# Polysketch attention and a multiplicative feed-forward block: the same 1179 steps dealt out in another order, with half of the first keys and S transferred first

## The chip, the cores and the metric

The kernel runs on one core of one Trainium2 chip. A core has five engines that matter here: TensorE (PE, the matmuls), VectorE (DVE), ScalarE (ACT), GpSimd (POOL) and SyncE (SP, which in this kernel only issues transfers). Each engine works through its own list of instructions in the order in which they stand, and waits on semaphores where it needs another engine's or a transfer's result. The metric is the device time of one execution in microseconds, as a median of several. Numbers of the trace come from one profiled execution, whose clock starts at the first instruction.

## The reference

```python
def phi(x):                                        # r = 8
    a = np.einsum('rd,bhsd->bhsr', S1, x)
    b = np.einsum('rd,bhsd->bhsr', S2, x)
    return np.einsum('bhsi,bhsj->bhsij', a, b).reshape(*x.shape[:-1], r * r)
q_p, k_p = (phi(q), phi(k))                        # q, k, v: (4, 4, 1088, 32)
kv = np.einsum('bhsf,bhsd->bhfd', k_p, v)
z = np.sum(k_p, axis=2)
num = np.einsum('bhsf,bhfd->bhsd', q_p, kv)
den = np.einsum('bhsf,bhf->bhs', q_p, z)[..., None] + 1e-06
attn = (num / den).astype(np.float32)
x = attn.transpose(0, 2, 1, 3).reshape(4 * 1088, 128)
h = (x @ w1) * (x @ w2) @ w3                       # w1, w2: 128 x 1024; w3: 1024 x 1024
out = (h @ w_out).astype(np.float32)               # w_out: 1024 x 128
```

The four batches are independent in the attention part; the feed-forward part treats all 4352 rows of x alike. The weights arrive as double-precision words and are turned into single precision in the kernel.

## The kernel before

`make_steps` defines 1179 small named steps, each of one or a few instructions. The names say what a step belongs to:

- `k0` to `k3` are the keys of the four batches. The biggest magnitude of a batch is found on ACT (`max`, L207), the keys are split into a leading part on a grid and a rest (`lead`, `rest`, L651), a Gram matrix is made of them on PE (`gram`, L659), and from it the sums `N` that later steps need; beside that the keys are transposed (`tr`, `kT`), multiplied with S (`ab`), squared into their 64 features (`kp`, L677), and multiplied with the values (`kv0` to `kv3`, L769, and `kvr`).
- `q0` to `q6` and `qr` are pieces of the queries: projections, the features `phi` (L1208, L1509), the denominator `rc`, and at the end `xT`, the transposed rows x. `q0` and `q1` are 512 rows of batch 0 each, made in another way than the later ones.
- `w0` to `w10` turn the weights into single precision (`c` and `m` on ACT, `j` on DVE, `a` on POOL), and `f0` to `f7` multiply w3 with w_out once (L534), so that the feed-forward part is only (x w1)(x w2) w3o.
- `g0` to `g3` are the feed-forward part for 512 rows each of batches 0 and 1: `a` (L1799) and `b` (L1809) are matmuls against a 128-column block of w1 and of w2, `c` (L1804) copies the first product out of PSUM, `m` (L1815) multiplies the two on DVE, and `o` (L1835) is the matmul with w3o. `gr` is the same for the 256 rows that are left of all batches, with `o` at L1824 and `oT` at L1858.
- `h4` and `h6` are the feed-forward part of batches 2 and 3, 1024 rows each, by a scheme of seven half-size products in place of eight. The products `a1` to `a7` use rows 0 to 63 of the PE array and `b1` to `b7` rows 64 to 127 (L1673); `P1` to `P7` use columns 0 to 63 or 64 to 127 (L1759). Two neighbours on opposite halves run side by side. Copies (L1680), additions (L1685), multiplications (L1707, L1712) and sums (L1727 to L1742) on ACT, DVE and POOL stand between `a`/`b` and `P`, and a chain of DVE additions `k2` to `k9` (L1776 to L1785) ends it.
- `warm0` to `warm11` are filler matmuls on zeros (L255), 53 in all, 27 of them in `warm0`.

What sets the order of the work is a table written out by hand or by a planner: the string `ORDER` lists all step names once. The steps are traced in that order, and every instruction is chained behind the one traced before it on the same engine (L1892 to L1904), so `ORDER` fixes the list of each of the five engines. Three sets of names choose an engine: a step in `POOL` runs on GpSimd and otherwise on VectorE; a PSUM copy in `CPV` runs on VectorE and otherwise on ScalarE. `SLOTS` deals the buffers: for each kind of tile it is a string in which the n-th character says which buffer the n-th tile of the kind takes, so a step may have to wait for the last reader of that buffer.

Transfers are issued from SP, but for the two halves of batch 0's keys (`k0.load0`, `k0.load1`, L560), which are issued from ACT. Each big transfer on SP waits until the one four places ahead of it has landed (`UNDER_WAY`), and every transfer waits for the one eight places before it, since transfers share eight semaphores.

## Time and profile before

| what | value |
|---|---|
| median of 3 runs | 245.85 us (245.68 to 246.19) |
| the profiled execution's span, first to last instruction | 244.1 us |
| median less span: what lies around it | 1.75 us |
| PE busy | 236.2 us, 97% of the span |
| DVE busy | 206.7 us, 85% |
| POOL busy | 161.9 us, 66% |
| ACT busy | 123.5 us, 51% |
| mean granted TensorE clock | 0.998 |
| first matmul of the feed-forward part (`g0.4a`) | starts at 27.42 us |
| last `a`/`b`/`o` matmul ends | about 240.6 us |

The page cuts the span into 40 slices with the busy share of each engine in tenths, names the chain of work that ended last, and lists the costliest groups of instructions by source line. A table by windows of time gives the busy time of each engine in each stretch; the timeline lists the instructions one by one with the idle time ahead of each and what ended it ("issue" is idle time for which the profile shows no waited-for event). A PE record's end is modelled; how long a matmul holds the array is read from the start of the next one.

### The profile page before, as it was taken

The page shows a single profiled execution, that of the slowest core. Times are in us where ns is not written, and L with a number is a line of the kernel's source. Part 1 is how long each engine was busy: PE and PEld are TensorE (multiplying, and loading weights), DVE is VectorE, ACT ScalarE, POOL GpSimd, SP SyncE. Part 2 cuts the span into 40 slices and gives each one's busy share as a digit, 9 for nine tenths or more (in the row PEclk, how much of TensorE's full clock was granted, in tenths as well). Part 3 has the DMA queues.
Part 4 walks back from the last instruction along what each step waited for, and adds up shares of the span by engine and source line. Part 5 has one row for each costly group of instructions (what it writes and reads, how often), then busy time and mean ns, then how long its engine had stood idle before and what let it go on. Part 6 is the DMA issues. An engine that isn't in the chain of part 4 may idle for free.

```text
span 244.1 us, 6745 instructions
## 1 busy us (share of the span) xinstructions
PE 236.2 (97%) x2724; PEld 129.8 (53%) x2724; DVE 206.7 (85%) x421; ACT 123.5 (51%) x246; POOL 161.9 (66%) x203
## 2 busy tenths in 40 slices
...
GB/s 201 265 143 325 181 227 190 6 197 224 220 141 251 188 217 190 59 1 3 3 0 0 4 0 3 59 113 3 1 0 0 0 3 0 0 1 3 12 90 93
DMA packets 31935, 22.06 MB, mean 90 GB/s; under 512 B 21280, under 2 KB 26528, under 8 KB 31904
## 3 DMA queue, kind: packets, MB, share of 16 engines
...
q8 instruction: 21, 0.34, 0.6%
q10 hardware_dynamic: 544, 0.52, 0.6%
...
## 4 chain that ended last, share of the span: by engine, by line
PE 87%; DMA 5%; ACT 2%; POOL 2%; DVE 1%; issue 1%; POOLq 0%; SPq 0%
PE b_ps L1809 12%; PE ps_o L1835 12%; PE ps_X L1673 11%; PE a_ps L1799 11%; PE ps_o L1759 10%; PE ps_w3o L534 6%; PE ps_Y L1673 6%; PE ps_Z L1673 3%; PE ps_g L659 2%; PE ps_x L1527 2%; PE ps_ac L1374 2%; DMA qh<-in_q_dram 2%; DMA k<-in_k_dram 2%; PE ps_or L1824 2%; POOL ph L1208 1%; PE idle_ps L255 1%
## 5 line engine op out<-in xcount | busy, mean ns | idle before, releaser
L1673 PE MATMUL ps_X<-xd,wv 64*128 64x512 f32 x112 | 36.3, 593 | 0.0
L1799 PE MATMUL a_ps<-xT,w 128*128 128x512 f32 (+1 forms) x80 | 36.1, 562 | 0.0
L1809 PE MATMUL b_ps<-xT,w 128*128 128x512 f32 (+1 forms) x80 | 35.6, 555 | 0.0
L1804 ACT COPY ffa<-a_ps 128x512 f32<-128x512 f32 (+1 forms) x38 | 20.1, 540 | 29.2 <-PE a_ps L1799 26.7
L1707 POOL TENSOR_TENSOR hc<-hc 128x512 f32<-128x512 f32 x16 | 20.7, 1304 | 15.7 <-DVE hc L1685 15.5
L1835 PE MATMUL ps_o<-ab,w3o 128*128 128x512 f32 x64 | 29.6, 600 | 0.0
L1680 ACT COPY hc<-ps_X 128x512 f32<-128x512 f32 x38 | 21.3, 590 | 16.1 <-PE ps_X L1673 12.9
L1815 DVE TENSOR_TENSOR ab<-ffa,b_ps 128x512 f32<-128x512 f32 (+1 forms) x40 | 23.9, 623 | 4.9 <-PE b_ps L1809 4.1
L501 POOL TENSOR_TENSOR w3c<-w3c,cv_m 128x512 int32<-128x512 int32 x16 | 21.2, 1344 | 4.2 <-DVE w3c L495 4.1
L1673 PEld LDWEIGHTS ps_X<-xd,wv 64*128 64x128 f32 x112 | 14.9, 186 | 13.1 <-issue 10.9
L1799 PEld LDWEIGHTS a_ps<-xT,w 128*128 128x128 f32 x80 | 14.1, 189 | 13.9 <-issue 8.8
L1809 PEld LDWEIGHTS b_ps<-xT,w 128*128 128x128 f32 x80 | 14.4, 190 | 13.1 <-issue 8.1
L1673 PE MATMUL ps_Y<-xd,wv 64*128 64x512 f32 x48 | 19.7, 594 | 0.0
L1835 PEld LDWEIGHTS ps_o<-ab,w3o 128*128 128x128 f32 x64 | 11.6, 190 | 13.4 <-issue 13.0
L534 PEld LDWEIGHTS ps_w3o<-wo,w3T 128*128 128x128 f32 x128 | 15.3, 192 | 2.4 <-issue 2.4
L534 PE MATMUL ps_w3o<-wo,w3T 128*128 128x128 f32 x128 | 15.7, 276 | 0.0
L1759 PE MATMUL ps_o<-hc,w3o 128*64 128x512 f32 x32 | 15.1, 595 | 0.0
L1759 PE MATMUL ps_o<-tt,ws 128*64 128x512 f32 x32 | 13.7, 594 | 0.0
L1680 ACT COPY hc<-ps_Y 128x512 f32<-128x512 f32 x14 | 8.1, 592 | 9.7 <-PE ps_Y L1673 6.6
L263 ACT ACTIVATE cv_c<-raw 128x1024 f32<-128x1024 f32 (+1 forms) x13 | 13.0, 1014 | 0.0
L1540 ACT COPY xd<-ps_x 64x256 f32<-64x256 f32 x24 | 8.8, 367 | 7.2 <-PE ps_o L1835 6.8
...
## 6 DMA issues: line engine op xcount, KB each, us to landing
...
raw<-in_moe_w_dram SPq DMA_DIRECT2D x4, 512.0 KB, 5.8
...
k<-in_k_dram SPq DMA_DIRECT2D x3, 512.0 KB, 5.1
v<-in_v_dram SPq DMA_DIRECT2D x2, 512.0 KB, 6.1
...
```

What stands on the lines that cost most here:

```text
L263: act.activation(dst, hi.bitcast(F32), ACT.Prelu, scale=2.0 ** -112, alpha=-2.0 ** 32)
L501: pool.tensor_tensor(d, d, x["m"][:, i * 512:(i + 1) * 512], ALU.add)
L534: pe.matmul(t["o"], w3T[ko][:, c], wo[:, c], start=c == 0, stop=c == NC - 1)
L1673: pe.matmul(x[bank], stat(j, u)[:, i * 128:(i + 1) * 128], rows(j, u), start=new, stop=True, tile_position=(u * 64, 0), skip_group_check=True)
L1680: cp(n(y))(x[k], x[bank])
L1707: on(f"h{g}.{i}m{k}").tensor_mul(both[0][k], both[0][k], both[1][k])
L1759: pe.matmul(acc_o[bank][half[0]:half[1]], w(i), x(i), start=n == 1, stop=n == (2 if j == 3 else 4), tile_position=(0, half[0]), skip_group ...
L1799: pe.matmul(x["a"][:, :w], w_of(0, c), xT[g][:, c0:c0 + w], start=True, stop=True)
L1804: cp(f"g{g}.{c}{su}c")(x["s"][:, :w], x["a"][:, :w])
L1809: pe.matmul(x["b"][:, :w], w_of(1, c), xT[g][:, c0:c0 + w], start=True, stop=True)
L1815: dve.tensor_mul(ab_sb[g, c][:, c0:c0 + w], x["s"][:, :w], x["b"][:, :w])
L1835: pe.matmul(o_ps[g], w3o[:, c], ab_sb[g, c], start=n == 1, stop=n == NC)
```

## The change

The code of the steps is the same. What differs is six of the strings of `SLOTS`, the sets `POOL` (90 names before, 88 now: 32 left, 30 joined) and `CPV` (17 before, 20 now), and the whole of `ORDER`, which holds the same 1179 names in another order. The number of fillers is the same, too.

```diff
 SLOTS = {
     "b": 
-        "012345670214657210671306537457462512346127340273014526045721472352140327540542370673245716"
...
+        "012345670123457361203270534526506451021657206572143063275430125416214572614576305416273054"
...
-    "q_m": "0110110",
-    "raw": "010212120211221",
-    "s": "012345671252360063202461521024214",
-    "x": "012012201110",
+    "q_m": "0101101",
+    "raw": "012010201210210",
+    "s": "012345674062315470625130724635017",
+    "x": "012101201201",
...
 POOL = set("""
-    g4.oS g5.oS g6.oS g7.oS h4.0T1 h4.0T2 h4.0T3 h4.0m12 h4.0m22 h4.1T2 h4.1m11 h4.1m12 h4.2m11
-    h4.2m12 h4.2m22 h4.3m11 h4.s2 h4.s4 h6.0T2 h6.0m11 h6.0m12 h6.0m22 h6.1T2 h6.1T3 h6.1m11 h6.1m12
-    h6.1m22 h6.2T1 h6.2T4 h6.2m11 h6.3T3 h6.3m11 h6.s1 h6.s2 h6.s4 k0.Nf k0.Nh k0.Nr k0.kp1 k1.Nr
-    k1.kp1 k2.kp0 k2.kp1 k2.rest0 k3.kp0 k3.kp1 q0.al q0.p01 q0.phi1 q0.sca q1.al q1.bs q1.p12
-    q1.phi q1.sca q2.bs q2.p2 q2.phi0 q2.sc q2.sl q3.al q3.bs q3.p01 q3.p12 q3.p2 q3.phi0 q3.sc
-    q4.al q4.bs q4.nn q4.p01 q4.p2 q4.phi0 q4.sl q6.al q6.nn q6.p01 q6.phi1 q6.sc q6.sl qr.al qr.bs
-    qr.p12 qr.p2 s.KS s.Pp s.blk s.blkh s.low s.rest
+    g4.oS g5.oS g6.oS g7.oS h4.0T1 h4.0T3 h4.0T4 h4.0m12 h4.0m22 h4.1T1 h4.1T3 h4.1m11 h4.1m12
+    h4.1m22 h4.2m11 h4.2m12 h4.s2 h6.0m11 h6.0m12 h6.0m22 h6.1T1 h6.1T3 h6.1T4 h6.1m12 h6.1m22
+    h6.2T2 h6.2T3 h6.2m12 h6.2m22 h6.s1 h6.s2 h6.s4 k0.Nf k0.Nh k0.rest1 k1.Nr k1.kp0 k1.kp1
+    k1.rest0 k2.Nr k2.kp1 k2.rest0 k3.Nr k3.rest0 q0.al q0.p2 q0.phi1 q0.sca q1.al q1.bs q1.p12
+    q1.p2 q1.phi q2.al q2.bs q2.p12 q2.p2 q2.phi0 q2.sc q2.sl q3.al q3.bs q3.p12 q3.sc q3.sl q4.bs
+    q4.nm q4.nn q4.p01 q4.p2 q4.phi0 q4.phi1 q4.sc q4.sl q6.al q6.p01 q6.p12 q6.p2 q6.phi1 q6.sl
+    qr.al qr.p01 qr.p12 qr.sc s.AR s.blkh s.rest s.sum
 """.split())
 
 ACTS = set("k0.lead1 k1.lead0".split())
 
 CPV = set("""
-    g0.0c g0.1c h4.1ac h4.1ad h6.1bc h6.2ad k0.kT1 k1.kvc k2.kT1 k2.kq k3.kT0 k3.kT1 k3.kq q0.xc0
-    q0.xc1 q6.xT0 q6.xT2
+    g0.2c g0.3c g0.4c g0.5c g1.1c g1.7c g2.2c g2.6c g3.2c g3.3c h4.1ai h4.1bc h4.1be h4.2ad h4.3bd
+    h6.0ae k3.kvc kr0.kT q0.xc1 q4.xT3
 """.split())
 
 CPG = set("""
...
 ORDER = """
-c.zeros warm0 q0.load c.ident s.four c.act c.mask s.zero k0.zero v0.zero s.load k0.load0 k0.loadr q0.restT q0.tr
-k0.load1 s.words kr0.load k0.tr1 s.pair s.low s.lead s.sum k0.max0 k0.max1 warm1 q0.max k0.tr0 warm2 kr0.tr kr0.kT
...
+c.zeros warm0 k0.zero k0.load0 c.act warm1 warm4 s.load q0.load warm11 k0.load1 s.words s.pair c.mask c.ident k0.loadr
+s.low s.lead s.sum k0.max0 warm5 s.rest s.four kr1.load s.T s.tc k0.max1 s.P s.R kr1.tr k1.zero q0.tr kr0.load q1.tr
...
-gr.5o0 g6.oS g6.st g7.oS g7.st gr.6m gr.6o1 gr.1m gr.6o0 gr.1o0 gr.5o1 gr.oT0 gr.1o1 gr.oT1 gr.st1
+gr.0o1 gr.6o0 gr.5o1 gr.4o1 gr.0o0 gr.4o0 gr.oT0 gr.oT1 gr.st1
```

Since the rows of `ORDER` tell little, three places show what it does to the lists of the engines. A row names the source line, the instruction, the tile written and the tiles read, and the shape.

**SP, the first transfers.** `qh` is the queries of batch 0 (first row) and 1, `s_raw` is S, `k` a batch's keys (128x4x256 the bulk, 64x4x32 the last 64 positions), `kr` the last positions of two batches side by side, `raw` raw weights, `v` the values. Before:

```order
L975 DMA qh<-in_q_dram 128x1088
L287 DMA s_raw<-in_S_dram 8x32 x2
L572 DMA k<-in_k_dram 64x4x32
L609 DMA kr_161<-in_k_dram 64x4x32 x2
L430 DMA raw<-in_moe_w_dram 128x512 x2
L582 DMA v<-in_v_dram 128x4x256
L593 DMA v<-in_v_dram 64x4x32
L560 DMA k<-in_k_dram 128x4x256
```

And now:

```order
L287 DMA s_raw<-in_S_dram 8x32 x2
L975 DMA qh<-in_q_dram 128x1088
L572 DMA k<-in_k_dram 64x4x32
L609 DMA kr_187<-in_k_dram 64x4x32 x2
L609 DMA kr_211<-in_k_dram 64x4x32 x2
L560 DMA k<-in_k_dram 128x4x256
L430 DMA raw<-in_moe_w_dram 128x512 x4
L572 DMA k<-in_k_dram 64x4x32
L582 DMA v<-in_v_dram 128x4x256
L593 DMA v<-in_v_dram 64x4x32
```

S now stands ahead of the first queries, and the values of batch 0 have moved behind the keys of batch 1 and all of w1 and w2. On ACT the first half of batch 0's keys (L560) now stands ahead of the table load and of the first small copy (L248), the second half behind them; before, both halves stood behind. The fillers follow suit: 39 now stand ahead of the first other matmul, 27 did before.

**PE, the half-size products of `h4`.** Each of these matmuls uses rows 0 to 63 (a product `a`) or rows 64 to 127 (a product `b`) of the array; `ps_X`, `ps_Y`, `ps_Z` are the accumulators, `xd` the rows x or their differences, the last name the weights. Before, the ten products 2b5, 3a2, 2b7, 2a7, 3b2, 2a5, 2b3, 3a6, 3b6, 3a5:

```order
L1673 MATMUL ps_Y_2699<-xd_2413,wv_2398 128x512
L1673 MATMUL ps_Z_2703<-xd_2376,wv_2316 128x512
L1673 MATMUL ps_X_2644<-xd_2355,wv_2612 128x512
L1673 MATMUL ps_X_2651<-xd_2355,wv_2612 128x512
L1673 MATMUL ps_Z_2708<-xd_2376,w12_81 128x512
L1673 MATMUL ps_Y_2714<-xd_2413,wv_2398 128x512
L1673 MATMUL ps_Y_2699<-xd_2590,w12_81 128x512
L1673 MATMUL ps_X_2687<-xd_2421,wv_2398 128x512
L1673 MATMUL ps_X_2689<-xd_2421,wv_2398 128x512
L1673 MATMUL ps_Y_2724<-xd_2413,wv_2398 128x512
```

And now the ten products 2a3, 3a6, 3b7, 2b6, 2b5, 2a7, 3a5, 3a7, 3b3, 2b7:

```order
L1673 MATMUL ps_Y_2688<-xd_2590,wv_1841 128x512
L1673 MATMUL ps_X_2683<-xd_2573,wv_2394 128x512
L1673 MATMUL ps_X_2657<-xd_2424,wv_2307 128x512
L1673 MATMUL ps_X_2690<-xd_2573,wv_2394 128x512
L1673 MATMUL ps_Y_2722<-xd_2494,wv_2394 128x512
L1673 MATMUL ps_X_2659<-xd_2424,wv_2307 128x512
L1673 MATMUL ps_Y_2730<-xd_2494,wv_2394 128x512
L1673 MATMUL ps_X_2683<-xd_2424,wv_2307 128x512
L1673 MATMUL ps_Y_2693<-xd_2590,w12_81 128x512
L1673 MATMUL ps_X_2690<-xd_2424,wv_2307 128x512
```

Taken two by two, the ten of before are one `a` and one `b` each time (b a, b a, b a, b a, b a). The ten of now are a, a b, b b, a a, a b, b: 2a3 is followed by another `a`, and so on. Counted over both `a`/`b` and `P` from the front and closing a pair wherever two neighbours use opposite halves, the 168 half-size matmuls of before make 84 pairs with none left over; those of now make 80 pairs and leave 8 alone (2a3, 2b6 and 3a5 of `h4`, 0b1 of `h6`, 1P4 and 1P2 of `h4`, 3P7 and 1P3 of `h6`).

**PE, the last passage from half-size rows to half-size columns in `h6`.** `a_ps` and `b_ps` are the products of the 256 remaining rows (`gr`), `ps_o` the output of the column products. Before:

```order
L1673 MATMUL ps_X_2920<-xd_2493,wv_2612 128x512
L1809 MATMUL b_ps_3022<-xT_2543,w12_81 128x256
L1799 MATMUL a_ps_3024<-xT_2543,w12_81 128x256
L1809 MATMUL b_ps_3029<-xT_2543,w12_81 128x256
L1799 MATMUL a_ps_3031<-xT_2543,w12_81 128x256
L1799 MATMUL a_ps_3037<-xT_2543,w12_81 128x256
L1799 MATMUL a_ps_3041<-xT_2543,w12_81 128x256
L1809 MATMUL b_ps_3047<-xT_2543,w12_81 128x256
L1673 MATMUL ps_X_2967<-xd_2493,wv_2612 128x512
L1673 MATMUL ps_X_2957<-xd_2493,wv_2612 128x512
L1759 MATMUL ps_o_3055<-hc_2910,ws_2409 64x512
L1759 MATMUL ps_o_3057<-hc_2831,w3o_83 64x512
```

And now:

```order
L1673 MATMUL ps_X_2948<-xd_2498,wv_2307 128x512
L1673 MATMUL ps_X_2953<-xd_2498,wv_2307 128x512
L1809 MATMUL b_ps_3028<-xT_2554,w12_81 128x256
L1799 MATMUL a_ps_3032<-xT_2554,w12_81 128x256
L1799 MATMUL a_ps_3036<-xT_2554,w12_81 128x256
L1799 MATMUL a_ps_3038<-xT_2554,w12_81 128x256
L1809 MATMUL b_ps_3043<-xT_2554,w12_81 128x256
L1809 MATMUL b_ps_3048<-xT_2554,w12_81 128x256
L1759 MATMUL ps_o_3052<-hc_2907,w3o_83 64x512
L1759 MATMUL ps_o_3057<-tt_2968,ws_2389 64x512
```

Before, two products of `h6` stand behind the seven of `gr`; now all products of `h6` stand ahead of six of `gr`. Behind this place the column products (L1759) were interrupted twice by matmuls of `gr` before, and now run through to the last; 25 matmuls of `gr` (9 `a`/`b`, 16 `o`) stand behind it, against 18 (6 and 12).

More of the change, by code (lines that the diff above doesn't have):

```diff
@@ new lines @@
+s.blkh s.RC k0.gram0 kr0.kT k0.gram1 k0.tr0 q0.rm q0.A0 s.KS k1.load k0.lead1 kr0.ab s.AR k0.ab1 k1.tr1 kr1.kT warm3
+q0.C0 kr0.abc q0.sma q0.sta q1.max q1.l2 k0.rest1 q0.sha q1.l1 q0.sla q0.C0t k0.gram2 kr0.kp q1.rm q0.sca w1.load
+w0.load k1.loadr k0.gram3 k0.gram4 k0.Gm k0.Gt k0.kT0 k0.Ga k0.ab0 k0.abc0 k0.T0 k0.Gb k0.Gc k0.Ta k1.tr0 k0.N0 k0.kp0
+w1.c1 k0.T1 w1.c0 k0.Tb q1.C0 q0.al k0.Na k0.Nh q0.phi0 k0.Tc k0.N1 k0.abc1 v0.load w0.c0 warm2 k0.Nb w1.m0 kr1.ab
+v0.loadr warm9 warm7 q0.pt0 k0.Nf q0.A1 q0.phi1 k0.kp1 q0.smy q0.sty k1.kT1 q1.A0 k0.kv0 q1.sm q0.C1 k1.max q1.load
@@ new lines @@
+k0.kv3 q0.C1t k0.kv1 q0.pc0 k0.kv2 k0.kvr q0.shy q0.sly q1.C1 kr1.abc q0.scy q0.p01 q1.st w1.m1 q0.p2 k0.kvc q0.p12
+k0.kvm k1.kT0 q0.pt1 q0.dn q0.de k0.kzt q0.rc k2.zero k0.kz k0.kqt q0.pc1 w1.j1 w9.load k2.loadr w1.j0 q0.x0 q0.x1
+q0.xs0 w0.j0 q0.xs1 q0.xc0 q0.xc1 kr1.kp k1.lead0 q0.xt1 k0.kq kh2.load q0.xt0 k1.ab w1.a0 q0.xT1 q0.xT0 w1.a1 w0.m0
+g0.5b g0.0a q3.tr q3.max q1.sh g0.5a q2.tr w0.c1 w6.load q1.sl q1.Ct g0.7b g0.7a w0.m1 q1.sca g0.6a k1.abt q1.scy
+k1.rest0 k2.load k1.gram0 k1.gram1 q1.p01 q2.max w0.a0 g0.5c k1.gram2 k2.kT0 w9.m k1.gram3 g0.6c w0.j1 k2.kT1 k1.gram4
```

132 lines of the change are left out of this document (61 added, 71 removed).

## The prediction

> **What bounds the kernel now.** I read the page first.
>
> ```profile
> span 244.1 us, 6745 instructions
> PE 236.2 (97%) x2724; PEld 129.8 (53%) x2724; DVE 206.7 (85%) x421; ACT 123.5 (51%) x246; POOL 161.9 (66%) x203
> ```
>
> PE works for 236.2 of 244.1 us. The median is 245.85, so 1.75 us lie around the span; I take these as unchanged and make the sum on the span. The table by windows says where the other 7.9 us are (columns: window, its length, busy us and instructions of each engine, clock, DMA share, GB/s).
>
> ```profile
> 0.00:6.00 6.00, 4.91 (x29) 3.61 (x29) 1.43 (x7) 1.88 (x4) 2.52 (x30) 1.00 0.71 203
> 6.00:18.00 12.00, 11.41 (x256) 9.79 (x257) 9.38 (x29) 10.09 (x26) 7.14 (x14) 1.00 0.74 199
> 18.00:27.40 9.40, 8.16 (x224) 6.18 (x225) 7.17 (x24) 7.16 (x17) 5.55 (x9) 1.00 0.81 264
> 27.40:45.00 17.60, 17.36 (x292) 8.76 (x292) 15.37 (x39) 12.80 (x28) 11.90 (x14) 1.00 0.77 186
> 45.00:50.00 5.00, 3.84 (x186) 2.74 (x175) 4.62 (x13) 2.26 (x3) 2.62 (x5) 1.00 0.05 10
> 50.00:100.00 50.00, 50.00 (x710) 27.70 (x709) 46.47 (x98) 31.76 (x54) 36.54 (x32) 1.00 0.82 205
> 200.00:220.00 20.00, 20.00 (x94) 10.01 (x90) 19.39 (x31) 9.69 (x19) 15.52 (x12) 1.00 0.00 0
> 235.00:244.10 9.10, 5.56 (x38) 5.03 (x36) 4.30 (x10) 1.01 (x3) 2.28 (x3) 0.95 0.44 82
> ```
>
> PE idles 1.09 us in the first 6, 0.59 to 18, 1.24 to 27.4, 0.24 to 45, 1.16 to 50; from 50 to 235 it is never idle, at full clock, and 3.5 us after its last matmul belong to the last copy and store. So there are four things that an order can change: the head (before 27.4 us), these few stalls, how long PE's own work takes, and the tail. Of the 85% that DVE is busy, nothing shows on PE in the middle; but 19.39 of 20 from 200 on is close.
>
> **The head.** The timeline shows who waits there (start, length, engine, line; in brackets the idle time ahead and what ended it):
>
> ```profile
> 1.93 0.73 SPq L572 DMA_DIRECT2D k<-in_k_dram  x1
> ...
> 5.13 0.26 ACT L263 ACTIVATE sk_c<-s_raw 8x64 f32<-8x64 f32 x1 [2.91 <-DMA s_raw<-in_S_dram]
> ...
> 6.41 0.68 ACT L207 ACTIVATE k_abs<-k 128x576 bf16<-128x576 f32 x1 [0.87 <-POOL sk_m L313]
> ```
>
> S was used at 5.13, when ACT had waited 2.91 us for it; issued ahead of the first queries (544 KB) it comes, I estimate, about 1 us sooner. But the long ACT chain starts with k_abs (L207), which reads 576 columns, so also the last 64 positions of the keys (L572). Those are issued from SP right behind the queries before and now; half of the keys coming sooner doesn't move them. I estimate its start at 6.1 to 6.4. From there, laying the steps of the new lists end to end with the lengths that the same steps have in this trace, I find the sums N 0.5 us sooner, the first query features 1.1 sooner, the denominators 0.4 sooner. But three weight conversions now stand ahead of the copies of x on DVE, where this one stood,
>
> ```profile
> 25.44 0.36 DVE L466 TENSOR_SCALAR w<-cv_c 128x512 int32<-128x512 int32 x1
> ```
>
> and 2×0.4 more takes that back. PE's rows:
>
> ```profile
> 20.35 0.69 PE L769 MATMUL ps_kv<-kp,v 128*32 128x64 f32 x34 [0.91 <-issue]
> ...
> 38.37 0.33 PE L1246 MATMUL ps_ph<-ident,ph 128*128 128x128 f32 x1 [0.24 <-POOL ph L1208]
> ```
>
> By these lists the first feed-forward matmul, at 27.4 before, comes at 27.4 again; the 0.91 in the first row and what follows it stay. **Head: 0**, bounds −1.5 (about half of the 2.92 us that PE idles to 27.4 given back) and +1.5 (below, values late).
>
> **Fillers.** Nine of them started within 1.15 us:
>
> ```profile
> 4.54 1.15 PE L255 MATMUL idle_ps<-zeros 128*128 128x256 bf16 x9
> ```
>
> That is 0.13 each at most, and with the last one's tail off 0.11. All 53 lay in the head before, in time that PE had; 3 of them now stand behind 27.4, between matmuls that follow each other: **+0.33**.
>
> **The stall at 38 us** waited for features on POOL (row above, 0.24). Those are issued earlier relative to PE now: **−0.24**, bounds −0.24 and +0.24 (as long again).
>
> **The stall at 45.8 us.**
>
> ```profile
> 45.83 1.16 issue
> ```
>
> ```profile
> q8 instruction: 21, 0.34, 0.6%
> ```
>
> "issue" in the middle of a Gram matrix, where PE starts 186 instructions in 5 us, against 710 in 50 later. The second row is the page's count of a queue for instructions: 21 transfers, 0.34 MB, so 16 KB each, for some 5400 PE instructions. So one block of about 256 is eaten in a few microseconds there, faster than elsewhere, and PE waits for the next. In the new order the same small matmuls stand side by side again (the query projections L1374 and the Gram matrix of batch 2), only other blocks end there. **0**, bounds −1.16 and +1.16. [...]
>
> **The passages between tile shapes.** PE's rows where it leaves half-size rows for full tiles and comes back:
>
> ```profile
> 156.67 0.59 PE L1673 MATMUL ps_X<-xd,w 64*128 64x512 f32 x1
> 156.68 0.59 PE L1673 MATMUL ps_X<-xd,wv 64*128 64x512 f32 x1
> 157.10 0.59 PE L1673 MATMUL ps_X<-xd,w 64*128 64x512 f32 x1
> ```
>
> ```profile
> 215.60 0.59 PE L1673 MATMUL ps_X<-xd,wv 64*128 64x512 f32 x2
> 216.13 0.70 PE L1809 MATMUL b_ps<-xT,w 128*128 128x256 f32 x2
> 216.66 0.59 PE L1799 MATMUL a_ps<-xT,w 128*128 128x256 f32 x2
> ```
>
> Inside a shape, starts are 0.43 apart (156.67, 157.10). Across the passage it is 0.53 (215.60 to 216.13), and the first two behind it take 0.53 in place of 0.43. So a passage costs about 0.2. In the feed-forward part the lists hold 55 passages before, 49 now; five of the six lie in the last 30 us. **−1.0**, bounds −1.2 (six at 0.2) and −0.6 (six at the 0.1 that only the first half of such a passage costs); I stay near the first, since most are of the kind shown.
>
> **Moves between DVE and POOL.** Ten copies of the feed-forward part now run on DVE, two before; the squares kp of the keys lose three places on POOL; three key rests go there.
>
> ```profile
> L1804 DVE COPY ffa<-a_ps 128x512 f32<-128x512 f32 x2 | 1.4, 678 | 0.0
> L677 DVE TENSOR_TENSOR kp<-kab 128x1024 f32<-128x1024 f32 x1 | 1.2, 1206 | 0.0
> ```
>
> The first two are +5.4 (8×0.678) and +3.6 (3×1.206) on DVE; the rests and six key copies leave it, and adding every moved step at the length of its like I get +2 to +3 in all. It lies beside PE: DVE is idle 3.5 us from 50 to 100 alone. **0**; where the cover is gone is a rival below.
>
> **The half-size products.** Pairs start 0.01 apart, and the next pair of records follows 0.43 later; a product has two records, so a pair holds the array for 0.86 and a lone one for the same. The new order, read strictly, leaves 8 alone: 88 turns for 84, +3.43. But this trace shows PE starting a later matmul ahead of one that waits for its tile:
>
> ```profile
> 74.58 0.34 PE L659 MATMUL ps_g<-kk 128*32 128x64 f32 x8
> 74.72 0.22 PE L659 MATMUL ps_g<-k,kk 128*32 128x32 f32 x4
> ```
>
> The list has kk, k of head 0, kk, k of head 1 and so on, each head on its own 32 columns; on the chip all eight kk records (four heads, two each) start before the first k. A k that waits did not hold up the next head's kk. If halves of rows behave like that, a waiting product lets the other half's next one pass, and all 168 fit into 84 turns: **0**, bounds 0 and +3.43.
>
> **The tail.**
>
> ```profile
> 230.97 0.68 DVE L1776 TENSOR_TENSOR oc<-oc,ps_o 64x512 f32<-64x512 f32 x1
> ...
> 237.28 1.90 DVE L1815 TENSOR_TENSOR ab<-ffa,b_ps 128x256 f32<-128x256 f32 x5
> ...
> 238.16 2.39 PE L1824 MATMUL ps_or<-w3o,ab 128*128 128x128 f32 x20
> ```
>
> From k2 to the first multiplication (L1815) the DVE chain takes 6.31 us. Now k2 waits for a product about 1.6 us ahead of the end of the last column product, so the five multiplications end from 5.2 to 6.7 us behind that end. PE has 9×0.43 + 5×0.22 = 5.0 us of work that needs none of them, then 11 outputs of 0.22 (20 records in 2.39). The first waits to 5.3: **+0.3**, bounds 0 and +1.1.
>
> **Sum:** +0.33 − 0.24 − 1.0 + 0.3 = −0.6: span 243.5, median **245.2**. Under 0.2% (0.49 us) can't be told from no change.
>
> **The rivals.**
>
> *A lone half holds up the list.* Then +3.43 − 0.6 = +2.8: 248.7, slower. It decides as soon as a second product on the same half, waiting, stops the one behind it; then each of the 8 lone products costs half a turn. For it: row halves are not column tiles of 32, and no list of before shows them alone. Against it: the Gram rows. [...]
>
> *The values come late.* They landed ahead of the first keys of batch 1 and half of the weights; now the keys of batch 1 and all of w1 and w2 stand ahead.
>
> ```profile
> raw<-in_moe_w_dram SPq DMA_DIRECT2D x4, 512.0 KB, 5.8
> ```
>
> Four of these make 2.1 MB, with the first queries, two batches of keys, the small pieces and the values themselves 4.4 MB. At 264 GB/s (the window from 18) from 2 us on that ends at 18.7; at the 200 of the windows to 18 and then 264, at 21.1. The values' matmul (20.35) will want them at about 20. I expect 19; at 21.1, PE is held 1 us and the DVE work behind it, packed to 40 us, some more: +1.5 to +2 on the sum, 246.7 to 247.2.
>
> *The head shrinks.* If S a microsecond sooner and the feature rows 1.1 sooner carry through to the first feed-forward matmul: −1.2 more, 244.0.
>
> *DVE in the last third.* `h6` gains one sum and one multiplication on DVE and loses a copy (0.68).
>
> ```profile
> L1742 DVE TENSOR_TENSOR tt<-tt,hc 128x512 f32<-128x512 f32 x7 | 4.7, 680 | 0.0
> L1707 DVE TENSOR_TENSOR hc<-hc 128x512 f32<-128x512 f32 x8 | 6.7, 842 | 0.0
> ```
>
> That is +0.84 against 0.61 idle from 200 to 220. Then PE waits where it never did and the passages' gain is used up: 246.0.
>
> **How the numbers follow.** Chances: the sum holds 0.45 (its own range 244.3 to 246.2), lone halves 0.16, values late 0.17, shorter head 0.12, DVE 0.10. Faster than by 0.2%: 0.28 of the sum's case, all 0.12 of the head's, 0.01: 0.41. Within: 0.13 + 0.03 + 0.07 = 0.23. Slower: 0.04 + 0.16 + 0.14 + 0.02 = 0.36. The range 243.4 to 248.3 takes in the bounds of the head and of late values and leaves out the full price of lone halves (0.13) and the longest gain (0.05).
>
> **What would show it.** First feed-forward matmul at 27.4 ± 1; the values' matmul not held by a transfer; half-size records always in pairs 0.43 apart, also around 2a3; fewer passages of 0.53; three filler records late; no idle PE from 50 to 230. Half-size records alone for 0.86 make the prediction wrong, as does any idle time of PE in the middle that DVE or POOL ends.

## The result, and the profile after

The changed kernel takes 258.49 us (median of 4 runs, 257.16 to 260.37) against 245.76 for the kernel before beside it on the same chip. The ratio is 1.0537, with a 95% interval from 1.0485 to 1.0589. The forecast was 245.2 and no slower than 248.3: it was wrong in sign and in size.

The page of the changed kernel, its span and its engines:

```profile
span 255.0 us, 6749 instructions
PE 241.6 (95%) x2724; PEld 140.0 (55%) x2724; DVE 220.5 (86%) x429; ACT 120.0 (47%) x243; POOL 158.0 (62%) x198
```

The span grew by 10.9 us (244.1 before; the profiled execution is the shortest of the four, 257.16, so the medians lie further apart, 12.7). PE's busy time grew too, by 5.4, although it does the same 2724 matmuls: part of the loss is slower work, not idle time. The table by windows shows where (columns as in the prediction; the clock is the third number from the right):

```profile
6.00:18.00 12.00, 9.60 (x232) 8.39 (x229) 9.12 (x26) 8.44 (x21) 5.91 (x14) 1.00 0.83 273
18.00:30.66 12.66, 10.89 (x245) 8.15 (x244) 10.21 (x32) 10.11 (x25) 5.86 (x8) 0.87 0.67 177
30.66:68.89 38.23, 38.23 (x642) 19.52 (x642) 36.58 (x86) 26.93 (x43) 30.64 (x30) 1.00 0.91 227
68.89:72.50 3.61, 0.00 (x0) 0.00 (x0) 3.61 (x4) 0.22 (x2) 2.61 (x3) 1.00 0.91 185
72.50:79.62 7.12, 6.34 (x101) 3.30 (x102) 5.62 (x14) 3.65 (x9) 0.00 (x0) 0.52 0.81 196
200.00:220.00 20.00, 20.00 (x94) 11.39 (x92) 18.80 (x31) 9.32 (x19) 9.90 (x13) 1.00 0.00 1
```

The head ends 3.2 us later, and has a stretch at a lower clock. From 30.66 to 68.89 PE never idles: both stalls of the kernel before (38 and 45.8 us) are gone. Then PE idles 3.61 us in one piece, and the 7.1 us behind that run at half clock. In the timeline, the first feed-forward matmul, the first half-size product and the last outputs stand here:

```profile
30.66 1.10 PE L1809 MATMUL b_ps<-xT,w 128*128 128x512 f32 x2 [0.23 <-DVE xT L1291]
165.22 0.69 PE L1673 MATMUL ps_Y<-xd,wv 64*128 64x512 f32 x1
248.81 2.72 PE L1824 MATMUL ps_or<-w3o,ab 128*128 128x128 f32 x22 [0.27 <-DVE ab L1815]
```

With the same three places of the kernel before, the 10.9 us divide as follows.

| stretch | before | after | difference |
|---|---|---|---|
| to the first feed-forward matmul | 27.42 | 30.66 | +3.24 |
| from there to the first half-size product | 128.29 | 134.56 | +6.27 |
| from there to the end of the last matmul | 84.85 | 86.31 | +1.46 |
| behind it | 3.54 | 3.47 | -0.07 |

**The middle.** The page's costliest group names the wait:

```profile
L1809 PE MATMUL b_ps<-xT,w 128*128 128x512 f32 (+1 forms) x80 | 38.3, 584 | 3.8 <-ACT T_p L908 3.6
```

PE waits for a copy on ACT; that copy waits for VectorE, and VectorE's timeline beside GpSimd's shows why:

```profile
65.17 0.17 DVE L201 SCALAR_TENSOR_TENSOR T_t<-T_g,ps_T 32x32 f32<-32x32 f32 x1
65.38 6.16 DVE L204 SCALAR_TENSOR_TENSOR T_p<-T_g,T_t 32x32 f32<-32x32 f32 x1
65.49 1.94 POOL L1509 TENSOR_TENSOR ph<-s_al,s_bs 128x1024 f32<-128x1024 f32 x1
67.40 0.44 POOL L1426 TENSOR_TENSOR s_al<-s_hl 128x128 f32<-128x128 f32 x1
67.81 1.25 POOL L501 TENSOR_TENSOR w3c<-w3c,cv_m 128x512 int32<-128x512 int32 x1
69.03 2.47 POOL L501 TENSOR_TENSOR wo<-wo,cv_m 128x512 int32<-128x512 int32 x2
72.28 0.17 ACT L908 COPY T_p<-ps_T 32x32 f32<-32x32 f32 x1 [6.78 <-DVE T_p L904]
72.50 1.83 PE L1809 MATMUL b_ps<-xT,w 128*128 128x512 f32 x2 [3.61 <-ACT T_p L908]
```

L204 is the third instruction of `k2.Ta`, on a tile of 32x32. It lasts 6.16 us, the one of the same shape ahead of it 0.17. It ends at 71.54, 0.04 after the last of a row of GpSimd's instructions without a pause (69.03 + 2.47): six of them, with a short fill at 65.33 that isn't shown. The two instructions differ in one thing: L201 reads one operand from PSUM, L204 reads both from SBUF. The kernel before had the same thing in small, and the prediction made no use of it:

```profile
38.27 1.27 POOL L470 TENSOR_TENSOR w<-w,cv_m 128x512 int32<-128x512 int32 x1
38.59 0.99 DVE L204 SCALAR_TENSOR_TENSOR T_p<-T_g,T_t 32x32 f32<-32x32 f32 x1
```

Here, too, VectorE's instruction ends 0.04 after GpSimd's (39.58 and 39.54), but there GpSimd paused after one instruction.

The clock's part of the middle (one row a stretch of 3.41 us; PE's busy time is the second number, the clock the third from the right):

```profile
69.38:72.79 3.41, 0.29 (x1) 0.29 (x2) 3.41 (x5) 0.51 (x2) 2.12 (x2) 1.00 0.80 166
72.79:76.20 3.41, 2.64 (x58) 0.99 (x69) 2.96 (x5) 2.58 (x5) 0.00 (x0) 0.50 0.64 174
76.20:79.62 3.42, 3.42 (x58) 2.02 (x49) 2.37 (x9) 0.77 (x4) 0.00 (x0) 0.50 1.04 232
```

The stretch with next to no work is followed by two at half clock. Work done there takes double (a matmul of 512 columns lasts up to 1.22 us there, 0.59 elsewhere), so 6.06 us of busy PE (2.64 + 3.42) cost about 3.0 more than at full clock. 3.6 idle, 0.8 idle at 74.56 and 3.0 of clock are 7.4; the two stalls that are gone take back 1.4: 6.0 of the 6.27.

**The head.** In the rows of the head, S is used at 3.63 (5.13 before), yet the maximum of the keys starts later:

```profile
3.63 0.26 ACT L263 ACTIVATE sk_c<-s_raw 8x64 f32<-8x64 f32 x1 [0.94 <-DMA s_raw<-in_S_dram]
6.81 0.68 ACT L207 ACTIVATE k_abs<-k 128x576 bf16<-128x576 f32 x1 [2.77 <-DMA kr<-in_k_dram]
16.45 0.22 PE L659 MATMUL ps_g<-k,kk 128*32 128x32 f32 x1 [1.33 <-issue]
```

`k_abs` comes 0.40 later than before (6.41), the stall inside the first Gram matrix is 1.33 (0.41 before), and a second one follows at 24.03 (0.83; before, 0.91 at 20.35). By their times these "issue" stalls are PE waiting for its own instructions: each of the four ends 1.3 to 1.5 us after one of the 16 KB instruction transfers has come in (15.02 and 22.58 in this trace, 12.94 and 18.94 before).

**The end** is told with the points of the prediction.

### The profile page after: what moved, and what is told of

Read it like the earlier page. It is cut to its first block, busy times and chain, and to the rows that moved or that the text cites. A ratio compares the mean times of both kernels' runs of the same rounds, so it can differ in the third digit from the quotient of the medians.

```text
span 255.0 us, 6749 instructions
## 1 busy us (share of the span) xinstructions
PE 241.6 (95%) x2724; PEld 140.0 (55%) x2724; DVE 220.5 (86%) x429; ACT 120.0 (47%) x243; POOL 158.0 (62%) x198
## 4 chain that ended last, share of the span: by engine, by line
PE 84%; DVE 6%; DMA 3%; issue 2%; POOL 1%; SPq 1%; ACT 1%; DVEq 0%
PE a_ps L1799 12%; PE ps_o L1835 11%; PE ps_X L1673 11%; PE b_ps L1809 10%; PE ps_o L1759 10%; PE ps_Y L1673 6%; PE ps_w3o L534 6%; PE ps_g L659 3%; PE ps_Z L1673 3%; PE ps_x L1527 2%; PE ps_ac L1374 2%; DMA raw<-in_moe_w_dram 2%; PE ps_or L1824 1%; DMA kr<-in_k_dram 1%; PE ps_kv L769 1%
## 5 line engine op out<-in xcount | busy, mean ns | idle before, releaser
L1809 PE MATMUL b_ps<-xT,w 128*128 128x512 f32 (+1 forms) x80 | 38.3, 584 | 3.8 <-ACT T_p L908 3.6
L1673 PE MATMUL ps_X<-xd,wv 64*128 64x512 f32 x112 | 39.4, 595 | 0.0
L1804 ACT COPY ffa<-a_ps 128x512 f32<-128x512 f32 (+1 forms) x30 | 15.2, 532 | 34.4 <-PE a_ps L1799 28.0
L1680 ACT COPY hc<-ps_X 128x512 f32<-128x512 f32 x36 | 19.8, 596 | 18.7 <-PE ps_X L1673 17.1
L1707 POOL TENSOR_TENSOR hc<-hc 128x512 f32<-128x512 f32 x14 | 18.0, 1304 | 14.8 <-DVE hc L1685 14.7
L1673 PEld LDWEIGHTS ps_X<-xd,wv 64*128 64x128 f32 x112 | 18.0, 186 | 9.6 <-issue 3.2
L1673 PE MATMUL ps_Y<-xd,wv 64*128 64x512 f32 x48 | 21.3, 591 | 0.0
L1497 POOL COPY nz<-nz 32x8 f32<-32x8 f32 x32 | 14.4, 451 | 1.4
L1540 ACT COPY xd<-ps_x 64x256 f32<-64x256 f32 x28 | 10.3, 367 | 10.6 <-PE ps_x L1527 10.2
L1759 PE MATMUL ps_o<-hc,w3o 128*64 128x512 f32 x32 | 14.7, 597 | 0.0
L1759 PE MATMUL ps_o<-hc,ws 128*64 128x512 f32 x32 | 14.2, 594 | 0.0
L1759 PE MATMUL ps_o<-tt,ws 128*64 128x512 f32 x32 | 12.9, 595 | 0.0
```

The lines of the kernel that those rows point to most:

```text
L1497: pool.tensor_copy(s["es"][i * 32:(i + 1) * 32, t * nT:(t + 1) * nT], s["e2"][t * 32:(t + 1) * 32])
L1673: pe.matmul(x[bank], stat(j, u)[:, i * 128:(i + 1) * 128], rows(j, u), start=new, stop=True, tile_position=(u * 64, 0), skip_group_check=True)
L1680: cp(n(y))(x[k], x[bank])
L1707: on(f"h{g}.{i}m{k}").tensor_mul(both[0][k], both[0][k], both[1][k])
L1759: pe.matmul(acc_o[bank][half[0]:half[1]], w(i), x(i), start=n == 1, stop=n == (2 if j == 3 else 4), tile_position=(0, half[0]), skip_group ...
L1804: cp(f"g{g}.{c}{su}c")(x["s"][:, :w], x["a"][:, :w])
```

## The experiments

All times below stand beside runs of the kernel before on the same chip: 245.71 (first four), 245.39 (next four) and 245.22 (last four).

### e1_again: the changed kernel once more

No edit.

> The changed kernel itself, a second execution. If the 6.16 us that one small DVE instruction of k2.Ta (L204) took at 65.4 us belongs to the order of the lists, it is there again, 5 to 7 us long, together with about 4 us of idle PE and two stretches of 3.4 us at half the granted clock behind it. If it was an accident of one execution, the instruction takes 0.2 to 1.5 us here and the time is near 250 us.

258.75 us, one run. L204 lasted 6.17 us again, PE's gap was 3.62, with half clock from 72.1 to 82.3. In the head half clock came at another place (10.66 to 14.08), and the first feed-forward matmul at 31.80. So the middle is a property of the order, while the head differs by about a microsecond between two executions of the same kernel. The half clock behind the gap lasted 10.24 us here and 6.83 in the first profile.

### e2_mid: shorten GpSimd's run

Three additions of weights on GpSimd stand behind a later one.

```diff
 ORDER
-... k1.kq k2.N0 w9.a1 q2.pT0 w2.a0 g1.4c ... k2.Nb w2.a1 g1.4m ... w7.c w4.a0 q3.p12 ...
+... k1.kq k2.N0 q2.pT0 g1.4c ... k2.Nb g1.4m ... w7.c w4.a0 w9.a1 w2.a0 w2.a1 q3.p12 ...
```

> The changed kernel with one edit: on GpSimd the three weight additions w9.a1, w2.a0, w2.a1 (1.25 us each, 67.8 to 71.5 us) stand behind w4.a0, which has to wait for DVE, so GpSimd pauses at about 67.8. Theory 1 (a DVE instruction with all operands in SBUF is held off as long as GpSimd goes from one instruction to the next without a pause): L204 of k2.Ta ends at about 67.8 and takes 2.4 us, PE idles 0.5 us or less there, the granted clock stays whole, and the time falls by 6 to 8 us to about 251. Theory 2 (DVE waited for a transfer or an instruction fetch that ended at 71.45): it still takes 6 us, and the time stays at 257 to 260.

The timeline of that kernel:

```profile
66.43 2.51 DVE L204 SCALAR_TENSOR_TENSOR T_p<-T_g,T_t 32x32 f32<-32x32 f32 x1
66.54 1.95 POOL L1509 TENSOR_TENSOR ph<-s_al,s_bs 128x1024 f32<-128x1024 f32 x1
68.45 0.45 POOL L1426 TENSOR_TENSOR s_al<-s_hl 128x128 f32<-128x128 f32 x1
79.21 1.16 ACT L207 ACTIVATE k_abs<-k 128x1152 bf16<-128x1152 f32 x1 [7.59 <-POOL w3c L501]
81.18 2.08 PE L1799 MATMUL a_ps<-xT,w 128*128 128x512 f32 x2 [5.69 <-ACT xT L1549]
```

GpSimd's run is now over at 68.90, and VectorE's instruction ends at 68.94, after 2.51: it follows the end of the run again. The wait of `b_ps` is gone. But the time got longer, 261.55 (ratio 1.0656, 1.0601 to 1.0711), not about 251 as I had hoped. My own edit made a new wait: `k3.max` on ACT (79.21) takes over the buffer that `w9.a1` reads, so it stood 7.59 us behind the addition that I had moved, and the copies `xT` and PE's next product stood behind it. The mechanism was confirmed, the price of the stall was still open.

### e3_head: give the key rest back to VectorE

```diff
 POOL
-k0.rest1
+k0.kp1
```

> The changed kernel with k0.rest1 back on DVE and k0.kp1 back on GpSimd, as before the change. Theory 1 (in the head the slow rest on GpSimd, 1.55 us against 0.8, and kp1 on DVE, which holds k0.Nf on GpSimd up by 0.55 us, are late links): the first feed-forward matmul comes at 29.2 to 30.0 us in place of 30.7, and the time falls by 0.7 to 1.5 us. Theory 2 (the head is late because of an instruction fetch inside the Gram matrix and the half clock behind it, whatever runs elsewhere): the first feed-forward matmul stays within 0.4 us of 30.7.

259.04 us (ratio 1.0538, 1.0477 to 1.0599): no change. The first feed-forward matmul came at 32.40; the rest of the keys took 0.7 us less (1.55 us on GpSimd, 0.82 on VectorE), and an instruction of VectorE that it had held (`s_hla`, L204) took 0.72 in place of 1.57, but the Gram matrix behind it still stalled 1.10 on instructions, and a stretch at half clock came at 25.39. The engine of this step isn't what the head lost; the head came out even later than the 30.7 of the theory without a gain.

### e4_nofill: the kernel before without the later fillers

```diff
-WARM = [27, 2, 3, 4, 4, 4, 1, 2, 1, 1, 2, 2]
+WARM = [27, 0, 0, 0, 0, 0, 0, 0, 0, 0, 0, 0]
```

> The kernel before without 26 of its 53 filler matmuls (the 27 at the very start stay); the fillers compute nothing that is used. Theory 1 (the granted clock goes to one half for the next 3.4 us when PE idled more than about 1.2 us of a 3.4 us stretch, and the fillers prevent that): at least one stretch at half clock between 7 and 25 us, the first feed-forward matmul 1 to 4 us later than 27.4, the time 1 to 4 us longer. Theory 2 (fillers only take time that PE has): no change beyond 0.3 us.

One run took 248.89, the other three 252.79 to 255.55, against 245.71; I had expected 1 to 4 us more. The profile is of one of the three (254.41). A row of its table by windows:

```profile
24.74:28.15 3.41, 3.20 (x60) 2.65 (x63) 0.00 (x0) 1.24 (x4) 0.00 (x0) 0.50 0.44 141
```

The 26 fillers were not idle ballast of 0.11 us each: without them two stretches of the head fall to half clock in this profile, this one and the one from 11.09. By my estimate (some 5400 PE instructions in 21 transfers of 16 KB) they also shift which instructions stand in which of these blocks: a stall for instructions of 3.91 us came up at 21.04. Both together make the head 5.6 us longer in this execution (first feed-forward matmul at 33.02). The quickest run lost 3.2 us in all. Of that one there is no trace, so how much the fillers are worth by themselves isn't settled beyond this.

### e5_psum: one operand in PSUM

The decisive one. Only the place of one 32x32 operand changes; order, engines and GpSimd's run stay.

```diff
-            t = ps(tag, [shape[0], 2] + shape[1:], name)
+            t = ps(tag, [shape[0], 3] + shape[1:], name); a["spare"] = t[:, 2]
 ...
-            m, t = sb("T_g", [D, H]), sb("T_t", [D, H, r])
+            m, t = sb("T_g", [D, H]), a["spare"] if b == 2 else sb("T_t", [D, H, r])
```

> The changed kernel with one operand of one instruction moved: the third instruction of k2.Ta on VectorE (L204, T_p<-T_g,T_t, 32x32, which lasted 6.16 us beside an unbroken run of GpSimd) reads T_t from spare columns of its PSUM tile in place of an SBUF buffer. Order, engines and all other buffers stay. Theory (two engines share a way to SBUF, and an instruction of VectorE with all operands in SBUF is held off until GpSimd pauses; one that reads PSUM is not): the instruction lasts 0.2 us, GpSimd runs through from 65 to 71.5 as before, the gap of 3.61 us ahead of b_ps is gone, and with it the half clock behind it: 6 to 7 us less, 251.5 to 252.8. Rival (GpSimd's run is only a bystander, VectorE waited for something else that the profile does not show): 6.2 us again, 258.5.

251.04 us (250.22 to 251.9; ratio 1.023, 1.0194 to 1.0266): 7.5 less than the changed kernel, just below the range I had set. The timeline of the same place:

```profile
66.67 0.17 DVE L204 SCALAR_TENSOR_TENSOR T_p<-T_g,ps_T 32x32 f32<-32x32 f32 x1
66.77 1.94 POOL L1509 TENSOR_TENSOR ph<-s_al,s_bs 128x1024 f32<-128x1024 f32 x1
66.85 0.71 DVE L720 STREAM_TRANSPOSE kT<-kh 128x512 f32<-128x512 f32 x1
67.66 0.17 ACT L908 COPY T_p<-ps_T 32x32 f32<-32x32 f32 x1 [0.88 <-DVE T_p L904]
...
70.33 2.48 POOL L501 TENSOR_TENSOR wo<-wo,cv_m 128x512 int32<-128x512 int32 x2
```

The instruction lasts 0.17 us, and GpSimd runs through from 66.6 to 72.8 as before. The row behind it adds that not every instruction of VectorE is held: the transpose L720 reads and writes SBUF, but has one input, and runs at once beside GpSimd, in 0.71 us (0.69 to 0.71 for the four of its shape in the kernel before). What was held here is the instruction with two inputs in SBUF. From the first feed-forward matmul (31.94) to the first half-size product (160.27) it is 128.33 us, 128.29 in the kernel before: the whole loss of the middle hung on this one operand. That is 6.2 us between the two profiles. The medians differ by 7.5; part of that fits the half clock behind the stall, which lasted 10.24 us in e1 and e3 and only 6.83 in the first profile.

The traces show who is held: the instruction lasted 6.16 and 6.17 us with two inputs in SBUF, 0.17 with one. That the two engines share a way to SBUF, as the theory has it, fits this, but no run shows the way itself. How long the instruction is held differs: here it waited until a run of six of GpSimd's instructions was over, but that is not so everywhere. Two places of the kernel before, each with VectorE's instruction and then GpSimd's row:

```profile
81.27 1.30 DVE L204 SCALAR_TENSOR_TENSOR G_a<-G_g,G_t 128x32 f32<-128x32 f32 x1
80.01 3.75 POOL L501 TENSOR_TENSOR w3c<-w3c,cv_m 128x512 int32<-128x512 int32 x3
87.12 1.19 DVE L204 SCALAR_TENSOR_TENSOR T_p<-T_g,T_t 32x32 f32<-32x32 f32 x1
87.01 3.59 POOL L501 TENSOR_TENSOR w3c<-w3c,cv_m 128x512 int32<-128x512 int32 x2
```

Both were held as well (0.18 to 0.19 without GpSimd), but got through in the middle of GpSimd's run: they end at 82.57 and 88.31, the runs at 83.76 and 90.60. There the wait was over when one of GpSimd's instructions was (at 82.52 and 88.27). Why the instruction at 65.38 had to wait for all of them, in every profile of the new order in which both its inputs lay in SBUF, these runs don't show.

### e6_headb and e7_both: the head of the kernel before

The first 180 steps in the order, with the engines and the buffers of the kernel before, then the rest in the new order; e7_both has e5's edit as well.

```diff
-ORDER = (all steps in the new order)
+ORDER = (before: c.zeros ... q0.xT1, its first 180 steps) + (the others in the new order)
```

> Order, engines and buffers of the kernel before up to the first feed-forward matmul (180 steps), and those of the changed kernel behind it; 32 buffers in the middle are dealt again so that this is possible. The head of before includes its order of transfers. Theory 1 (the changed head itself costs about 3.2 us: keys' maximum 0.4 later, longer stalls of PE's instruction fetch, one stretch of 3.4 us at half clock): the first feed-forward matmul at 27.4 +- 0.3, no half clock ahead of it, the stall of T_p at 65 to 70 stays, 255.3 (254.5 to 256). Theory 2 (the later start only shifts a wait that comes in the middle anyway): the first feed-forward matmul at 27.4, but PE idles some 3 us more behind it, and 258 to 259 as the changed kernel.

> Both edits together: the head of before and the one operand in PSUM. If the head's 3.2 us and the 6.2 us of the stall and the clock behind it are all that the change lost ahead of the half-size products, what is left is the 1.4 us that these products and the end took longer: 249 (248.2 to 250), and PE is not idle for more than 0.5 us at a time from 50 to 230. Rival (other waits of the new order come forward once these are gone): 251 or more, with gaps of PE in the middle whose place the profile then shows.

257.97 us (ratio 1.0512, 1.0476 to 1.0548) and 251.13 (1.023, 1.0201 to 1.0259): no gain over the changed kernel and over e5, so theory 2 of e6 and the rival of e7 came out. The first feed-forward matmul did come early, at 28.80 and 28.15, and no half clock stood ahead of it. But the new order does 12 steps of the weights, S, the keys and the queries ahead of that place which the old one does behind it, and they were now missing. In e7 PE idled 1.66, 1.11 and 1.39 us between 26.5 and 34.6, for a copy on ACT (`kq`), a weight (`w`, L466) and a feature of the queries (`s_hl`, L1157) on VectorE. A splice of two orders doesn't measure the head by itself. What it does confirm is the middle: with the stall (e6) and without it (e7) the difference is 6.8 us.

### e8_start: only the part that names the change

```diff
 ORDER (before)
-c.zeros warm0 q0.load c.ident s.four c.act c.mask s.zero k0.zero v0.zero s.load k0.load0 k0.loadr ...
+c.zeros warm0 k0.zero k0.load0 s.load q0.load c.ident s.four c.act c.mask s.zero v0.zero k0.loadr ...
```

> The kernel before with only the part that the change is named after: S and the first half of the first keys issued ahead of the first queries, the second half behind. All else as before. Theory (the ACT chain starts with the maximum of all keys, which waits for the last 64 positions, issued behind the queries either way): k_abs at 6.3 to 6.5, first feed-forward matmul at 27.2 to 27.6, 245.7 +- 0.4. Rival (earlier keys and S carry through): 244.5 or less. Rival (the later queries hold up the transposes): 246.5 or more.

247.12 us (median of 12 runs, 245.62 to 250.68), ratio 1.0062 (1.0038 to 1.0087): slower by about 1.5 us. My expectation of no change was wrong, and the second rival was right, though it is VectorE's list that is held up. Two rows:

```profile
7.59 0.25 DVE L979 STREAM_TRANSPOSE qT_rest<-qh 128x64 f32<-128x64 f32 x1 [6.65 <-DMA qh<-in_q_dram]
7.87 0.68 ACT L207 ACTIVATE k_abs<-k 128x576 bf16<-128x576 f32 x1 [3.75 <-DMA k<-in_k_dram]
```

The queries landed at 7.57 in place of 4.62, the last 64 positions of the keys, issued from the same queue behind them, at 7.76 in place of 6.31, and the maximum of the keys started 1.46 later. S was there at 3.71, but VectorE's list begins with the queries, so S waited for them. ACT issues the second half of the keys while its table load still runs, so both halves leave ahead of the queries (0.75 and 1.26, the queries at 1.53; in the changed kernel the same). What the keys gain is taken from the queries, and from the positions queued behind them.

### e9_first: that part undone in the changed kernel

e5's edit, and the first transfers as before.

```diff
 ORDER (changed)
-c.zeros warm0 k0.zero k0.load0 c.act warm1 warm4 s.load q0.load warm11 k0.load1 ...
+c.zeros warm0 k0.zero c.act warm1 warm4 q0.load s.load warm11 k0.load0 k0.load1 ...
```

> The changed kernel with T_t in PSUM (as in e5_psum), and with the part that names the change undone: the first queries issued ahead of S again, and both halves of the first keys together behind the table load. All lists of PE, VectorE and GpSimd stay. Theory (behind the first keys the queries land at 6.2 to 7.6 in place of 4.6, and the last 64 positions of the keys, queued behind them, with them; the maximum of the keys, on which the head hangs, starts at 6.6 to 7.9 in place of 6.4): k_abs at 6.3 to 6.5, the first feed-forward matmul 1 to 1.5 earlier than with e5_psum (at 30.4 to 30.9), 249.5 to 250.2. Rival (S sooner makes up for it in this order of the lists): no gain, 250.8 to 251.5.

250.83 us (ratio 1.0234, 1.0216 to 1.0252), e5's time: in the times the rival holds. The traces show both halves of the story, the first row from e5:

```profile
7.90 0.68 ACT L207 ACTIVATE k_abs<-k 128x576 bf16<-128x576 f32 x1 [3.85 <-DMA k<-in_k_dram]
```

and these from e9:

```profile
6.35 0.68 ACT L207 ACTIVATE k_abs<-k 128x576 bf16<-128x576 f32 x1 [0.75 <-DMA k<-in_k_dram]
7.99 0.68 ACT L207 ACTIVATE k_abs<-k 128x576 bf16<-128x576 f32 x1
15.26:18.67 3.41, 2.31 (x72) 2.05 (x60) 1.73 (x7) 0.85 (x4) 1.26 (x2) 1.00 0.61 170
18.67:22.08 3.41, 3.41 (x69) 2.52 (x68) 2.98 (x12) 3.27 (x10) 0.67 (x2) 0.50 0.93 284
```

The first maximum starts 1.55 sooner, as forecast. But in the new order a copy of S's chain (L346) stands between the two maxima on ACT, and S now comes later again; so the second starts only 0.66 sooner (8.65 in e5). In the end the first feed-forward matmul is 0.80 earlier (31.14), in a profile in which a stretch at half clock stands ahead of it in either kernel. Undone, that part costs the new lists as much as it gives them.

### e10_fillers: fillers where the head waits

e9's kernel and

```diff
-WARM = [27, 2, 3, 4, 4, 4, 1, 2, 1, 1, 2, 2]
+WARM = [27, 2, 3, 4, 4, 4, 9, 2, 1, 1, 2, 2]
```

> e9_first with 8 more fillers (9 in place of 1 in warm6), which stand where PE waits 0.89 us for the leading part of the keys. Theory (a stretch of 3.4 us in which PE idles more than about 1.2 is followed by one at half clock; the head of the changed kernel has one such stretch in nearly every profile): the half clock ahead of 20 us is gone, and the first feed-forward matmul comes 0.8 to 1.5 earlier than in e9_first, 248.3 to 249.3. Rival (the stalls of instruction fetch at 16 to 25 us bring the half clock about, which no filler can cover): half clock stays, within 0.3 of e9_first.

249.23 us, three of four runs from 248.97 to 249.45, one at 252.62; ratio 1.0196 (1.0149 to 1.0242). No half clock ahead of the end, and the first feed-forward matmul at 29.26, 1.88 earlier than e9's. Part of that is not the clock: the stalls for instructions were shorter, too (0.85 in the Gram matrix, 1.10 in e9; the second one, 1.11 in e9, did not come, and a wait of 0.32 for GpSimd stands near its place). Eight fillers also move the blocks, by the estimate of e4. That the fillers help is likely; how much by the clock and how much by the blocks isn't told apart, and the intervals of e9 and e10 overlap.

### e11_copies: copies of ACT at the start of h4

e10's kernel and

```diff
-... q6.xT0 g1.oT h4.s1 g3.1o q6.xT2 ... h4.0b1 h4.0ac h4.0a2 q6.xT1 g0.st ...
+... q6.xT0 q6.xT1 g1.oT h4.s1 g3.1o q6.xT2 ... h4.0b1 h4.0ac h4.0a2 g0.st ...
```

> e10_fillers with one step of ScalarE moved: q6.xT1 (four copies of 0.37 us) stands behind q6.xT0 again, not between the first copies of the half-size products. Theory (of the 1.4 us that the last third lost, 0.75 came in the first 4.2 us of h4, where PE's weight loads wait for copies of ScalarE that stand behind q6's): the row phase of h4 lasts 27.0 to 27.3 us in place of 27.8, and the time is 0.5 to 0.8 less than e10_fillers. Rival (the first products start later instead, since the copies ahead of them are longer now): the row phase is shorter, but h4 starts as much later, and the time is the same.

250.91 us (ratio 1.0227, 1.0208 to 1.0247): the theory was wrong, and the rival half right. Nothing was gained, and `h4` starts 1.2 us later, counted from the first feed-forward matmul. But the row phase did not get shorter either (27.96 in place of 27.79). PE now idles 1.06 us ahead of the first product, for which the profile names no cause, and 0.35 behind the first turn for ACT's copies of `xd`, which end at 160.85. The 1.7 us to e10 is not all from here: in this profile the head is 0.9 longer too (30.15) and has a stretch at half clock, and the intervals of e10 and e11 overlap.

### e12_tail: the uninterrupted columns, in the kernel before

```diff
 ORDER (before)
-... gr.3o1 h6.k1 gr.2o0 gr.2o1 h6.2P3 ... h6.0P3 gr.7o0 g4.st gr.0a gr.5b h6.k5 ... h6.1P3 ...
+... h6.k1 h6.2P3 ... h6.0P3 g4.st h6.k5 ... h6.1P3 gr.3o1 gr.2o0 gr.2o1 gr.7o0 gr.0a gr.5b ...
```

> The kernel before with one idea of the change alone: the column products of h6 run through to the last, without the two interruptions by matmuls of the 256 remaining rows (gr.3o1, gr.2o0, gr.2o1, gr.7o0, gr.0a, gr.5b stand behind h6.1P3). Theory (each passage between tile shapes costs 0.1 to 0.2; four are saved, and PE has more work of its own while VectorE ends its chain): 0.6 less, 244.8 against 245.4. Rival (a later multiplication or sum then ends the kernel): no gain or up to 0.5 more.

245.28 against 245.22 us, ratio 0.9994 (0.9979 to 1.0008): no difference. In the trace the passages did save 0.7 us, by the starts of PE's rows. But VectorE's chain `k2` to `k9` ends no sooner, and the last multiplications behind it now hold PE:

```profile
237.53 2.42 PEld L1824 LDWEIGHTS ps_or<-w3o,ab 128*128 128x128 f32 x20 [0.48 <-DVE ab L1815]
```

0.46 goes back into that wait. PE's part from the first half-size product on is 0.24 shorter, too little to tell.

## Why the prediction was wrong

**What bounds the kernel.** "From 50 to 235 it is never idle" was read correctly, and the conclusion that an order can only change four places was not: it can make a fifth. A PE that never waits shows that every cover held in this order, not how much is left of each.

**Moves between DVE and POOL: "It lies beside PE ... 0".** This is the step that failed, by 6.2 us of span and 7.5 of time (e5). I weighed sums of busy time of VectorE, +2 to +3 us against 3.5 idle. The price did not come from a sum. It came from one instruction that VectorE could not run while GpSimd ran, with ACT and PE behind it. The hint stood in the profile of before: L204 with 0.99 beside 0.17 for its neighbour, and with 1.30 and 1.19 further on. And the list of GpSimd would have told how large the wait can get: from L1509 to the second `wo` addition there are five instructions in a row that wait for nobody, 1.94 + 0.44 + 1.25 + 2.47 = 6.10 us.

**Fillers: "+0.33".** Three did stand late (first at 90.4, last at 134.1), and cost about that. But the term counted only their own time. e4 shows what they are for: without the later ones the head was 5.6 us longer in the profiled execution, and the quickest run 3.2.

**Head: "0", bounds -1.5 and +1.5.** Measured +3.24 in the first profile, +1.8 to +5.0 in those of e1 to e10 with the new head. The step that failed is "half of the keys coming sooner doesn't move them", with the maximum at 6.1 to 6.4. It started at 6.63 to 7.90 in the changed head (e8: 7.87 in the old one), since the queries ahead of the last 64 positions came later themselves. The rest is stalls for instructions, which I took as unchanged ("the 0.91 in the first row and what follows it stay"), and the stretch at half clock that follows some of them, for which the sum had no term.

| | before | after | e5 | e9 | e10 |
|---|---|---|---|---|---|
| first maximum of the keys starts | 6.41 | 6.81 | 7.90 | 6.35 | 6.32 |
| second one | 7.10 | 7.56 | 8.65 | 7.99 | 8.02 |
| stall for instructions in the Gram matrix | 0.41 | 1.33 | 0.46 | 1.10 | 0.85 |
| half clock ahead of 30 us from | none | 18.18 | 11.02 | 18.67 | none |
| first feed-forward matmul | 27.42 | 30.66 | 31.94 | 31.14 | 29.26 |

What remains in e10, 1.84, is not taken apart further.

**The stalls at 38 and 45.8 us.** Both gone: -0.24 as forecast, and the other at its lower bound, -1.16. In the sum they were outweighed.

**Passages: "-1.0".** About right as a mechanism: by the starts of PE's rows, the interruptions that fell away in `h6` had cost 0.8. As a gain on the time it was not right, since the wait that follows takes it back, here and in e12.

**Half-size products: "0", bounds 0 and +3.43.** The mechanism was right and the rival wrong. The rows of the changed kernel around a lone product:

```profile
183.25 0.59 PE L1673 MATMUL ps_Y<-xd,wv 64*128 64x512 f32 x1
183.29 0.66 PE L1673 MATMUL ps_X<-xd,wv 64*128 64x512 f32 x1
183.68 0.59 PE L1673 MATMUL ps_Y<-xd,wv 64*128 64x512 f32 x1
183.79 1.77 PE L1673 MATMUL ps_X<-xd,wv 64*128 64x512 f32 x6
```

The two halves run as two streams, each with a start every 0.43 us, 0.04 apart here and 0.24 at the end of the row phase. The list has 2a3, 3a6, 3b7 here; the record at 183.29 is 3b7's, and 3a6 starts behind it, at 184.11, when 2a3 has left its half. A lone product lets the streams drift by a tenth or so, and holds up nothing for half a turn: three of them in this phase cost 0.24, not 1.29.

**The row phase itself** had no term and cost 0.98 (27.80 against 26.82 us): 0.24 of drift and 0.75 in its first 4.2 us, where PE's weight loads wait for copies of ACT.

```profile
166.33 0.29 PEld L1673 LDWEIGHTS ps_X<-xd,wv 64*128 64x128 f32 x2 [0.72 <-ACT xd L1540]
169.41 0.18 PEld L1673 LDWEIGHTS ps_X<-xd,wv 64*128 64x128 f32 x1 [0.77 <-ACT hc L1680]
```

**Tail: "+0.3", bounds 0 and +1.1.** The wait ahead of the outputs is the 0.27 of the row at 248.81. With two waits for VectorE's chain ahead of it (0.30 in the next row, 0.31 at 245.57) and slower last outputs it is about 0.9.

```profile
244.97 0.30 PEld L1809 LDWEIGHTS b_ps<-xT,w 128*128 128x128 f32 x2 [0.30 <-DVE oc L1782]
```

**The rivals.** Values late: no. The bulk of them landed at 18.20, and their matmul (24.21) waited for no transfer. (The prediction's later sum has a slip: at 200 GB/s from 2 to 18 us and 264 behind that, 4.4 MB end at 22.5, not 21.1.) DVE in the last third: no. From 200 to 220 VectorE was busy 18.80 and PE 20.00. Shorter head: no, the other way round. Of the signs that I had named, "any idle time of PE in the middle that DVE or POOL ends" came true at 68.89; I had given it 0.10 in the last third, and nothing where it happened.
